# Attention and GELU MLP on one core: softmax denominators by way of a 96 x 16 reciprocal and DRAM, filler matmuls, and a reordered LayerNorm prologue

## The chip, the cores and the metric

The kernel runs on one core of one Trainium2 chip. The metric is device time in microseconds. A run more than 1.5% above the fastest of the same kernel is called slow. The rounds ran on chips 0, 3 and 8, so each ratio is to the kernel before in the same rounds, and medians of different rounds are compared only with care.

## The reference, cut to what matters

```python
x = A_x                                   # 1 x 2048 x 512
xn = _layernorm(x)
# attention: 32 heads of 16 for q, one shared k and v
p = softmax(einsum("bhqd,bkd->bhqk", q, k) * 16 ** -0.5)
o = einsum("bhqk,bkd->bhqd", p, v)
# MLP: 512 -> 1792 -> 512, gelu (tanh form), from the same xn
return x + merge_heads(o) @ wo + gelu(xn @ w1 + b1) @ w2 + b2
```

## The kernel before

Queries come in 4 blocks of 512, heads in 11 groups (ten of 3, one of 2), keys in 16 tiles of 128. That makes 4 x 11 x 16 = 704 steps. One step computes the scores of one key tile for the heads of a group, their exp, and the product with V:

```python
def scores(s):            # 17 active rows per head, heads side by side in row groups
    for j, h in enumerate(GROUPS[g]):
        mm(bank(3 * x + j), KT[q0:q0 + 17, ...], QT[q0:q0 + 17, ...], True, True, ..., tp=(q0, 0))
def exp(s):               # ACT, 128 x 1536
    act(lambda e: e.activation(E[:, s % NEB, 0:n * TBW], bank(3 * x, n), ACT.Exp, scale=0.25), ...)
def pv(s):                # 128 active rows, 32 columns per head, heads side by side in column groups
    for j, h in enumerate(GROUPS[g]):
        mm(pO[32 * j:32 * j + 32, :], V1[:, kt, :], E[:, s % NEB, ...], kt == 0, kt == NT - 1, ..., tp=(0, 32 * j))
```

V1 has a column of ones, so row 16 of each head's 32 rows of `pO` is its softmax denominator. After the 16th key tile the group is normalised. The first and the last instruction read `pO`, the reciprocal stands between them, and the next group's first product waits for all three:

```python
def o_evac(tb, g):
    n = 32 * len(GROUPS[g]); i = g % 2
    dve(lambda e: e.stream_shuffle(den[0:n, i, :], pO[0:n, :], [16] * 32), w=[B(6), ("den", i)])
    dve(lambda e: e.reciprocal(den[0:n, i, :], den[0:n, i, :]), r=[("den", i)], w=[("den", i)])
    dve(lambda e: e.tensor_tensor(oT[0:n, tb % 2, g, :], pO[0:n, :], den[0:n, i, :], ALU.mult),
        r=[("den", i)], w=[B(6), ("oT", tb % 2, g)])
```

The rest of the work (q of the next block, the MLP, the output projection) is a generator `misc()` of matmuls, of which the loop takes up to `PER_STEP = 2` per step. A block boundary yields "gap", and then the next step has none. I call a step with none of these matmuls an idle step.

```python
for s in range(NS):
    exp(s)
    if s + 2 < NS: scores(s + 2)
    pv(s)
    if kt == NT - 1: o_evac(tb, g); done[(tb, g)] = s
    # [cut: tanh of three MLP blocks on ACT when four are ready, gates two steps later]
    n = 0
    while mi_live and n < PER_STEP and s >= gap_until:
        k = next(mi)                      # [cut: end of the generator]
        if k == "gap": gap_until = s + 2
        else: n += 1
```

Of the kernel before, what the change touches and what calls it, by code (L numbers as in the profile page):

```python
# [7 lines left out]
ALU = mybir.AluOpType  # L8
AX = mybir.AxisListType

P = 128
# [101 lines left out]
def bass_parallel_sum__grouped_kv_mqa__dense_activation_gelu__prompt_kernel(  # L113
# [18 lines left out]
    H, Dh = 32, 16  # L132
    NT = S // P
    DT = D // P
    FT = F // P
    TBW = 512
    NTB = S // TBW
    GROUPS = [list(range(h, min(h + 3, H))) for h in range(0, H, 3)]
    NGR = len(GROUPS)
    NEB = 4  # L140
# [3 lines left out]
    with ExitStack() as es:  # L144
        def sb(shape, dtype, name):
            return es.enter_context(nc.sbuf_tensor(name, shape, dtype))
# [38 lines left out]
        sqq = sb([P, 2, TBW], bf, "sqq")  # L185
        mT = sb([32, 2, TBW], bf, "mT")
        E = sb([P, NEB, 3 * TBW], bf, "E")
        den = sb([96, 2, TBW], f32, "den")
        oT = sb([96, 2, NGR, TBW], bf, "oT")
        hb = sb([P, FT, TBW], bf, "hb")  # L190
        ub = sb([P, FT, TBW], bf, "ub")
# [5 lines left out]
        def bank(b, n=1):  # L197
            return pAll[:, b * 512:(b + n) * 512]
# [5 lines left out]
        def B(b):  # L204
            return ("bank", b)

        def dve(fn, r=(), w=()):
            return add("dve", fn, r, w)
# [4 lines left out]
        def pool(fn, r=(), w=()):  # L213
            return add("pool", fn, r, w)
# [14 lines left out]
        for i in range(8):  # L229
# [11 lines left out]
        pool(lambda e: e.affine_select(out=ident[:], in_=ident[:], compare_op=ALU.not_equal, fill=1.0, base=0,  # L241
                                       pattern=[[-1, P]], channel_multiplier=1), r=["ident"], w=["ident"])
        pool(lambda e: e.memset(wkp[:], 0.0), w=["wkp"])
        pool(lambda e: e.tensor_copy(wkp[:, :, :, 0:Dh], wk_s[:].unsqueeze(2).to_broadcast([P, DT, 4, Dh])),
             r=["wk_s", "wkp"], w=["wkp"])
        pool(lambda e: e.memset(mask4[:], 1.0), w=["mask4"])
        pool(lambda e: e.affine_select(out=mask4[:], in_=mask4[:], compare_op=ALU.is_ge, fill=0.0, base=0,
                                       pattern=[[-32, 4]], channel_multiplier=1), r=["mask4"], w=["mask4"])
# [2 lines left out]
        pool(lambda e: e.memset(ones[:], 1.0), w=["ones"])  # L251
        pool(lambda e: e.memset(sel8[:], 0.0), w=["sel8"])
        pool(lambda e: e.memset(selr[:], 0.0), w=["selr"])
        pool(lambda e: e.memset(V1[:], 0.0), w=["V1"])
        pool(lambda e: e.memset(V1[:, :, Dh:Dh + 1], 1.0), r=["V1"], w=["V1"])
        pool(lambda e: e.memset(wqp[:], 0.0), w=["wqp"])  # L256
        pool(lambda e: e.memset(wop[:], 0.0), w=["wop"])  # L257

        sel_diag = bass.AP(sel8[:].tensor, sel8[:].offset, [list(sel8[:].ap[0]), [33, 8], [8, 4]])

# [10 lines left out]
            dve(lambda e: e.tensor_copy(selr[:, :, 16:17], mask4[:].unsqueeze(2)), r=["mask4", "selr"], w=["selr"])  # L271


        def ln_batch(b):
            t0 = 4 * b
            for ti in range(t0, t0 + 4):
                dve(lambda e, ti=ti: e.bn_stats(stats[:, ti, :], x_sb[:, ti, :]), r=[("x", ti)], w=[("st", ti)])  # L277
            for ti in range(t0, t0 + 4):
                dve(lambda e, ti=ti: e.bn_aggr(mv[:, ti, :], stats[:, ti, :]), r=[("st", ti)], w=[("mv", b)])
            sl = slice(t0, t0 + 4)  # L280
            dve(lambda e: e.tensor_scalar(ve_b[:, sl], mv[:, sl, 1], 1e-5, None, ALU.add), r=[("mv", b)], w=[("ve", b)])
            act(lambda e: e.activation(std_b[:, sl], ve_b[:, sl], ACT.Sqrt), r=[("ve", b)], w=[("std", b)])
            dve(lambda e: e.tensor_copy(m_b[:, sl], mv[:, sl, 0]), r=[("mv", b)], w=[("mb", b)])
            dve(lambda e: e.reciprocal(rstd[:, sl], std_b[:, sl]), r=[("std", b)], w=[("rstd", b)])
            dve(lambda e: e.scalar_tensor_tensor(nmr[:, sl], m_b[:, sl], -1.0, rstd[:, sl], ALU.mult, ALU.mult),
                r=[("mb", b), ("rstd", b)], w=[("nmr", b)])
            for ti in range(t0, t0 + 4):
                if ti % 2 == 0:
                    act(lambda e, ti=ti: e.activation(xn[:, ti % 8, :], x_sb[:, ti, :], ACT.Identity,  # L289
                                                      bias=nmr[:, ti:ti + 1], scale=rstd[:, ti:ti + 1]),  # L290
                        r=[("x", ti), ("rstd", b), ("nmr", b)], w=[("xn", ti % 8)])
                else:
                    pool(lambda e, ti=ti: e.tensor_scalar(xn[:, ti % 8, :], x_sb[:, ti, :], rstd[:, ti:ti + 1],
                                                          nmr[:, ti:ti + 1], ALU.mult, ALU.add),
                         r=[("x", ti), ("rstd", b), ("nmr", b)], w=[("xn", ti % 8)])
                pT = bank(ti % 3)[:, 0:256].bitcast(bf)
                for d in range(DT):
                    add("pe", lambda e, ti=ti, d=d, pT=pT: e.transpose(  # L298
                        pT[:, d * P:(d + 1) * P], xn[:, ti % 8, d * P:(d + 1) * P], ident[:]),
                        r=[("xn", ti % 8), "ident"], w=[B(ti % 3)])  # L300
                act(lambda e, ti=ti, pT=pT: e.activation(  # L301
                    xnT[:, :, ti * P:(ti + 1) * P], pT.rearrange("p (k n) -> p k n", k=DT), ACT.Copy),
                    w=[B(ti % 3), ("xnT", b)])

        def k_block(b):
            bk = 3 + b % 2
            c = slice(b * TBW, (b + 1) * TBW)
            for d in range(DT):
                mm(bank(bk), wkp[:, d, :, :].rearrange("p a n -> p (a n)"), xnT[:, d, c], d == 0, d == DT - 1,
                   r=["wkp", ("xnT", b)], w=[B(bk)])  # L310
            act(lambda e: e.activation(KT[:, c], bank(bk), ACT.Identity, bias=krow[:, 0:1]),  # L311
                r=["krow"], w=[B(bk), ("KT", b)])
            dve(lambda e: e.tensor_tensor(sqk[:, b % 2, :], KT[0:Dh, c], KT[0:Dh, c], ALU.mult),
                r=[("KT", b)], w=[("sqk", b % 2)])
            mm(bank(5), ones[0:Dh, :], sqk[:, b % 2, :], True, True, r=["ones", ("sqk", b % 2)], w=[B(5)])
            dve(lambda e: e.tensor_reduce(kmax[:, b:b + 1], bank(5), AX.X, ALU.max), w=[B(5), "kmax"])
# [25 lines left out]
        def v_tiles(ts, first=False):  # L342
            for ti in ts:
                for d in range(DT):
                    mm(pO[:, ti * Dh:(ti + 1) * Dh], xnT[:, d, ti * P:(ti + 1) * P], wv_s[:, d, :], d == 0, d == DT - 1,
                       r=["wv_s", ("xnT", ti // 4)], w=[B(6)])

        ln_batch(0)
        consts_dve()
        ln_batch(1)  # L350
        k_block(0)
        dve(lambda e: e.tensor_copy(wqp[:, :, 0:8, 0:Dh], wq_s[:, :, 0:128].rearrange("p k (h n) -> p k h n", n=Dh)),
            r=["wq_s", "wqp"], w=["wqp"])
        ln_batch(2)
        k_block(1)
        ln_batch(3)
        q_first(0, 7)
        k_block(2)
        v_tiles(range(0, 12))
        k_block(3)  # L360
        dve(lambda e: e.tensor_reduce(R2[:], kmax[:], AX.X, ALU.max), r=["kmax"], w=["R2"])
        dve(lambda e: e.tensor_scalar(selrR[:], selr[:], R2[:, 0:1], 1.03, ALU.mult, ALU.mult),
            r=["selr", "R2"], w=["selrR"])
        q_first_m(0, 7)
        v_tiles(range(12, 16))
        q_first(1, 3)
        dve(lambda e: e.tensor_copy(V1[:, :, 0:Dh], pO[:, 0:NT * Dh].rearrange("p (t n) -> p t n", n=Dh)),
            r=["V1"], w=[B(6), "V1"])
# [21 lines left out]
        def pv(s):  # L390
            tb, g, kt = steps[s]
            for j, h in enumerate(GROUPS[g]):
                mm(pO[32 * j:32 * j + 32, :], V1[:, kt, :], E[:, s % NEB, j * TBW:(j + 1) * TBW],
                   kt == 0, kt == NT - 1, r=["V1", ("E", s % NEB)], w=[B(6)], tp=(0, 32 * j))

        def o_evac(tb, g):
            n = 32 * len(GROUPS[g])
            i = g % 2
            dve(lambda e: e.stream_shuffle(den[0:n, i, :], pO[0:n, :], [16] * 32), w=[B(6), ("den", i)])  # L399
            dve(lambda e: e.reciprocal(den[0:n, i, :], den[0:n, i, :]), r=[("den", i)], w=[("den", i)])  # L400
            dve(lambda e: e.tensor_tensor(oT[0:n, tb % 2, g, :], pO[0:n, :], den[0:n, i, :], ALU.mult),  # L401
                r=[("den", i)], w=[B(6), ("oT", tb % 2, g)])


        def q_batch(tb, hqs):
# [79 lines left out]
        def misc():  # L485
# [26 lines left out]
            for i in range(4):  # L512
                yield from part_tile(NTB - 1, i, range(LASTG))


        for j in range(3):
            n = len([g for g in GROUPS if len(g) > j])
# [7 lines left out]
        mi_live = True  # L525
        gap_until = 0
        gates = []

        scores(0)
        q_first_m(1, 3)  # L530
        scores(1)
        for s in range(NS):
            tb, g, kt = steps[s]
            exp(s)
            if s + 2 < NS:
                scores(s + 2)
            pv(s)
            if kt == NT - 1:
                o_evac(tb, g)
                done[(tb, g)] = s  # L540
            if tanh_ready and s >= gap_until and (len(tanh_ready) >= 4 or tanh_ready[-1] == FT - 1):
                fts = tanh_ready[:3] if tanh_ready[-1] != FT - 1 else tanh_ready[:3]
                del tanh_ready[:len(fts)]
                tanh(fts)
                gates.append((s + 2, fts))
            while gates and gates[0][0] <= s:
                gate(gates.pop(0)[1])
            n = 0
            while mi_live and n < PER_STEP and s >= gap_until:
                try:  # L550
                    k = next(mi)
                except StopIteration:
                    mi_live = False
                    break
                if k == "gap":
                    gap_until = s + 2
                else:
                    n += 1
        assert not gates and not tanh_ready
        for _ in mi:  # L560
            pass
# [39 lines left out]
```

## Time and profile before

| | before |
|---|---|
| median of 3 runs | 1356.33 us (1349.05 to 1361.22) |
| span of the profiled run | 1340.7 us |
| start to first exp / first to last exp / rest | 62.4 / 1259.4 / 18.9 us |
| mean granted TensorE clock | 0.578 of full |
| steps whose exp starts at half clock | 597 of 704 |

The page of the kernel before: span, busy time of the engines, the clock in 40 slices (tenths of full speed), and the chain of work that ended last, by engine and by line.

```profile
span 1340.7 us, 11668 instructions
PE 1061.3 (79%) x4964; PEld 208.6 (16%) x5029; DVE 447.0 (33%) x642; ACT 998.7 (74%) x758; POOL 17.4 (1%) x26
PEclk9655555555557865555556865555558655755557
PE 61%; ACT 19%; DVE 17%; issue 2%; POOL 1%; DMA 0%; DVEq 0%
```

No engine is full, and yet 97% of the chain lies on PE, ACT and DVE. The timeline of one group's end shows DVE's part. The columns are start in us, length in us, engine, line, operation and tiles; in brackets the idle time before and who ended it.

```profile
320.22 0.61 PE L222 MATMUL pAll<-E,V 128*32 128x512 bf16 x3
320.86 0.61 PE L222 MATMUL pAll<-QT,KT 17*128 17x512 bf16 x3
320.94 0.72 DVE L399 STREAM_SHUFFLE den<-pAll 96x512 f32<-96x512 f32 x1
321.70 3.35 DVE L400 RECIPROCAL den<-den 96x512 f32<-96x512 f32 x1
325.08 0.69 DVE L401 TENSOR_TENSOR oT<-pAll,den 96x512 bf16<-96x512 f32 x1
325.83 0.61 PE L222 MATMUL pAll<-E,V 128*32 128x512 bf16 x3 [4.36 <-DVE oT L401]
```

PE stands still for 4.36 us, because its next product needs the bank that DVE is still reading. The waits view has the total (us, times, longest):

```profile
ACT E L387 <- PE pAll L222: 277.1, 216, 4.6
PE pAll L222 <- DVE oT L401: 178.5, 43, 4.4
```

The second limit is the clock. This is a step with two other matmuls at half clock, PE alone:

```profile
395.71 0.61 PE L222 MATMUL pAll<-E,V 128*32 128x512 bf16 x3
396.26 1.03 PE L222 MATMUL pAll<-wop,oT 96*128 96x512 bf16 x2
397.23 0.61 PE L222 MATMUL pAll<-QT,KT 17*128 17x512 bf16 x3
397.77 0.61 PE L222 MATMUL pAll<-E,V 128*32 128x512 bf16 x3
```

From one product to the next it takes 397.77 - 395.71 = 2.06 us, and PE has no gap, while the exp of a step takes 1.45 us (median; it is 1.02 for the group of two heads). At full clock the same step is bound by ACT, at 1.33 us from exp to exp; here are five exps without a gap:

```profile
415.59 6.82 ACT L387 ACTIVATE E<-pAll 128x1536 bf16<-128x1536 f32 x5
```

ACT's own floor of the loop, worked out from exp spacings and tanh times of this trace, is 640 x 1.331 + 64 x 1.08 + 20 x 1.37 = 948 us; the loop takes 1259.

### The profile page before, as it was taken

The page shows a single profiled execution, that of the slowest core. Times are in us where ns is not written, and L with a number is a line of the kernel's source. Part 1 is how long each engine was busy: PE and PEld are TensorE (multiplying, and loading weights), DVE is VectorE, ACT ScalarE, POOL GpSimd, SP SyncE. Part 2 cuts the span into 40 slices and gives each one's busy share as a digit, 9 for nine tenths or more (in the row PEclk, how much of TensorE's full clock was granted, in tenths as well). Part 3 has the DMA queues.
Part 4 walks back from the last instruction along what each step waited for, and adds up shares of the span by engine and source line. Part 5 has one row for each costly group of instructions (what it writes and reads, how often), then busy time and mean ns, then how long its engine had stood idle before and what let it go on. Part 6 is the DMA issues. An engine that isn't in the chain of part 4 may idle for free.

```text
span 1340.7 us, 11668 instructions
## 1 busy us (share of the span) xinstructions
PE 1061.3 (79%) x4964; PEld 208.6 (16%) x5029; DVE 447.0 (33%) x642; ACT 998.7 (74%) x758; POOL 17.4 (1%) x26
## 2 busy tenths in 40 slices
PE   2588888788887888887888778888878888676788
PEld 1211111111111111111111111111111111111112
DVE  4323444432112135444311224443331113453112
ACT  3387778878867787787777867888878767877852
POOL 4000000000000000000000000000000000000000
PEclk9655555555557865555556865555558655755557
DMA  6000000000000000000000000000000000000000
GB/s 205 0 1 1 1 0 1 1 1 1 0 0 8 4 4 1 0 1 1 1 1 4 9 5 0 0 1 1 1 0 5 4 4 4 0 1 0 0 0 16
DMA packets 12882, 9.83 MB, mean 7 GB/s; under 512 B 5405, under 2 KB 12318, under 8 KB 12830
## 3 DMA queue, kind: packets, MB, share of 16 engines
q1 hardware_dynamic: 11774, 9.05, 2.2%
q8 instruction: 39, 0.64, 0.2%
q10 hardware_dynamic: 1056, 0.03, 0.0%
q14 instruction: 13, 0.11, 0.0%
HBM read 6.85 MB, written 2.10 MB: 7 GB/s over the span
## 4 chain that ended last, share of the span: by engine, by line
PE 61%; ACT 19%; DVE 17%; issue 2%; POOL 1%; DMA 0%; DVEq 0%
PE pAll L222 61%; ACT E L387 16%; DVE den L400 11%; DVE den L399 2%; DVE oT L401 2%; ACT ub L441 1%; PE pAll L298 0%; ACT xn L289 0%; ACT xnT L301 0%; POOL wop L257 0%; DVE stats L277 0%; DMA wk_s<-in_A_wk_dram 0%; POOL wqp L256 0%; ACT KT L311 0%; DVE outb L568 0%
## 5 line engine op out<-in xcount | busy, mean ns | idle before, releaser
L387 ACT ACTIVATE E<-pAll 128x1536 bf16<-128x1536 f32 (+1 forms) x704 | 953.8, 1425 | 285.9 <-PE pAll L222 277.1
L222 PE MATMUL pAll<-E,V 128*32 128x512 bf16 x2048 | 409.5, 575 | 178.5 <-DVE oT L401 178.5
L222 PE MATMUL pAll<-QT,KT 17*128 17x512 bf16 x2048 | 404.1, 567 | 39.3 <-ACT E L387 31.8
L400 DVE RECIPROCAL den<-den 96x512 f32<-96x512 f32 (+1 forms) x44 | 147.3, 3349 | 1.5
L222 PEld LDWEIGHTS pAll<-E,V 128*32 128x32 bf16 x2048 | 74.5, 100 | 466.0 <-issue 266.1
L222 PEld LDWEIGHTS pAll<-QT,KT 17*128 17x128 bf16 x2048 | 72.8, 97 | 464.4 <-ACT E L387 260.8
L222 PE MATMUL pAll<-xnT,w_sb 128*128 128x512 bf16 x196 | 102.3, 610 | 8.6 <-issue 8.6
L428 DVE TENSOR_SCALAR hb<-pAll,b1T 128x512 bf16<-128x512 f32 x56 | 42.0, 750 | 189.7 <-PE pAll L222 189.7
L222 PE MATMUL pAll<-w_sb,ub 128*128 128x512 bf16 x209 | 91.3, 534 | 5.4 <-issue 4.6
L399 DVE LOAD_MASK_SELECT den<-pAll x44 | 0.6, 14 | 240.3 <-PE pAll L222 240.3
L470 DVE TENSOR_TENSOR outb<-pAll,x_sb 128x512 bf16<-128x512 f32 x12 | 8.3, 692 | 178.4 <-PE pAll L222 178.4
L222 PE MATMUL pAll<-wop,oT 96*128 96x512 bf16 (+1 forms) x176 | 66.8, 468 | 0.0
L326 DVE CAST QT<-pAll 128x512 bf16<-128x512 f32 x32 | 22.1, 690 | 120.0 <-PE pAll L222 120.0
L222 PE MATMUL pAll<-xnT,wqp 128*128 128x512 bf16 x108 | 57.5, 621 | 3.7 <-issue 3.7
L413 DVE TENSOR_SCALAR mT<-pAll 32x512 int16<-32x512 int32 x30 | 20.4, 678 | 69.9 <-PE pAll L222 69.9
L446 DVE SCALAR_TENSOR_TENSOR ub<-ub,hb 128x512 bf16<-128x512 bf16 x56 | 35.4, 685 | 21.0 <-ACT ub L441 21.0
L298 PE MATMUL pAll<-ident,xn 128*128 128x128 bf16 x64 | 8.5, 310 | 33.2 <-ACT xn L289 29.8
L399 DVE STREAM_SHUFFLE den<-pAll 96x512 f32<-96x512 f32 (+1 forms) x44 | 31.7, 720 | 0.0
L401 DVE TENSOR_TENSOR oT<-pAll,den 96x512 bf16<-96x512 f32 (+1 forms) x44 | 30.2, 686 | 1.5
L441 ACT ACTIVATE ub<-ub 128x1536 bf16<-128x1536 bf16 (+1 forms) x20 | 27.9, 1393 | 0.1
L433 DVE TENSOR_TENSOR ub<-ub,hb 128x512 bf16<-128x512 bf16 x56 | 23.8, 426 | 1.9
L430 DVE TENSOR_TENSOR ub<-hb 128x512 bf16<-128x512 bf16 x56 | 23.8, 424 | 1.9
(69 smaller groups left out, 208.1 us busy)
## 6 DMA issues: line engine op xcount, KB each, us to landing
w_sb<-in_B_w_dram SPq DMA_DIRECT2D x2, 1792.0 KB, 12.5
x_sb<-in_A_x_dram SPq DMA_DIRECT2D x8, 256.0 KB, 4.5
out_dram<-outb SPq DMA_DIRECT2D x16, 128.0 KB, 1.7
QT<-mT SPq DMA_DIRECT2D x120, 1.0 KB, 1.6
wq_s<-in_A_wq_dram SPq DMA_DIRECT2D x1, 512.0 KB, 6.3
wop<-in_A_wo_dram SPq DMA_DIRECT2D x2, 176.0 KB, 5.5
wop<-in_A_wo_dram SPq DMA_DIRECT2D x1, 160.0 KB, 3.0
wk_s<-in_A_wk_dram ACTq DMA_DIRECT2D x1, 16.0 KB, 3.5
```

The costliest lines, as they stand in the source:

```text
L222: return add("pe", lambda e: e.matmul(o, l, rh, start=start, stop=stop, **kw), r, w)
L326: dve(lambda e: e.tensor_copy(QT[:, pq, hq, :], bank(bk)), w=[B(bk), ("QT", pq, hq)])
L387: act(lambda e: e.activation(E[:, s % NEB, 0:n * TBW], bank(3 * x, n), ACT.Exp, scale=0.25), w=[B(3 * x + i) for i in range(3)] + [("E", s ...
L399: dve(lambda e: e.stream_shuffle(den[0:n, i, :], pO[0:n, :], [16] * 32), w=[B(6), ("den", i)])
L400: dve(lambda e: e.reciprocal(den[0:n, i, :], den[0:n, i, :]), r=[("den", i)], w=[("den", i)])
L401: dve(lambda e: e.tensor_tensor(oT[0:n, tb % 2, g, :], pO[0:n, :], den[0:n, i, :], ALU.mult), r=[("den", i)], w=[B(6), ("oT", tb % 2, g)])
L413: dve(lambda e, hq=hq: e.tensor_scalar(mT[:, hq % 2, :].bitcast(i16), pM[0:32, :].bitcast(i32), 0.5 / 65536.0, float(0x1fc00000) / 65536.0 ...
L428: dve(lambda e: e.tensor_scalar(hb[:, ft, :], pM, b1T[:, ft:ft + 1], None, ALU.add), r=["b1T"], w=[B(7), ("h", ft)])
L430: dve(lambda e: e.tensor_tensor(ub[:, ft, :], hb[:, ft, :], hb[:, ft, :], ALU.mult), r=[("h", ft)], w=[("u", ft)])
L433: dve(lambda e: e.tensor_tensor(ub[:, ft, :], ub[:, ft, :], hb[:, ft, :], ALU.mult), r=[("u", ft), ("h", ft)], w=[("u", ft)])
L441: act(lambda e: e.activation(ub[:, f0:f0 + n, :], ub[:, f0:f0 + n, :], ACT.Tanh, scale=GELU_K), r=[("u", f) for f in fts], w=[("u", f) for ...
L446: dve(lambda e, ft=ft: e.scalar_tensor_tensor(ub[:, ft, :], ub[:, ft, :], 1.0, hb[:, ft, :], ALU.add, ALU.mult), r=[("u", ft), ("h", ft)], ...
```

## The change

The intent has three parts. Denominators: copy `pO` out in one instruction so that the bank is free, take the denominators of the group as 96 x 16 instead of 96 x 512 so that the reciprocal is short, and return them to all rows by DMA through DRAM. Fillers: bring each step to two matmuls so that PE stays busy and its clock up. Prologue: compute LayerNorm of the four batches without waiting for the key maximum, and keep long Pool memsets away from DVE copies (before, two copies took 3.89 and 3.37 us beside a memset of 4.82 us). It also has 12 matmuls that nobody reads (`warm`).

```diff
-def o_evac of before                    # [cut: shown above]
+def o_evac(tb, g):
+    dve(lambda e: e.tensor_copy(Of[0:32 * n, i, :], pO[0:32 * n, :]), w=[B(6), ("Of", i)])
+    row = Of[16:17, i, :]
+    dma("sp", den[0:32 * n, i, :], bass.AP(row.tensor, row.offset, [[32 * row.ap[0][0], n], [1, TBW]]), ...)
+def o_recip(tb, g):                     # 4 steps later
+    dve(lambda e: e.reciprocal(den[0:32 * n, i, :], den[0:32 * n, i, :]), ...)   # 96 x 16
+    dma("sp", rows, den[0:32 * n, i, :], f"d_rd{i}", ...)                        # to DRAM
+    for j in range(n):
+        dma("sp", rbc[32 * j:32 * j + 32, i, :], bass.AP(src.tensor, src.offset, [[0, 32], [1, TBW]]), ...)
+def o_norm(tb, g):                      # 10 steps later
+    dve(lambda e: e.tensor_tensor(oT[...], Of[...], rbc[...], ALU.mult), ...)
+def fill(s, n):
+    for _ in range(n):
+        mm(pO[96:128, :], V1[:, kt, :], E[:, s % NEB, 0:TBW], True, True, ..., tp=(0, 96))
 ...
             if kt == NT - 1:
                 o_evac(tb, g)
-                done[(tb, g)] = s
+                later.append((s + 4, ...o_recip...)); later.append((s + 10, ...o_norm, done...))
 ...
+            fill(s, PER_STEP - n)
 ...
-ln_batch(0); consts_dve(); ln_batch(1); k_block(0); <wqp copy>; ln_batch(2); k_block(1); ln_batch(3); ...
+ln_batch(0); x_T(0); ln_batch(1); x_T(1); consts_dve(); k_proj(0); ln_batch(2); x_T(2); k_proj(1); ln_batch(3); warm(8); x_T(3); warm(4); <wqp copy>; k_max(0); ...
```

The filler writes rows 96 to 127 of `pO`, which nobody reads.

More of the change, by code (lines that the diff above doesn't have):

```diff
@@ L187, in bass_parallel_sum__grouped_kv_mqa__dense_activation_gelu__prompt_kernel @@
         E = sb([P, NEB, 3 * TBW], bf, "E")
-        den = sb([96, 2, TBW], f32, "den")
+        Of = sb([96, 2, TBW], f32, "Of")
+        den = sb([96, 2, 16], f32, "den")
+        rbc = sb([96, 2, TBW], f32, "rbc")
+        rd_dram = nc.dram_tensor("rden_rows", [NTB * NGR, 3 * TBW], f32).ap()
         oT = sb([96, 2, NGR, TBW], bf, "oT")
@@ L243, in bass_parallel_sum__grouped_kv_mqa__dense_activation_gelu__prompt_kernel @@
         pool(lambda e: e.memset(wkp[:], 0.0), w=["wkp"])
-        pool(lambda e: e.tensor_copy(wkp[:, :, :, 0:Dh], wk_s[:].unsqueeze(2).to_broadcast([P, DT, 4, Dh])),
-             r=["wk_s", "wkp"], w=["wkp"])
         pool(lambda e: e.memset(mask4[:], 1.0), w=["mask4"])
@@ L253, in bass_parallel_sum__grouped_kv_mqa__dense_activation_gelu__prompt_kernel @@
         pool(lambda e: e.memset(selr[:], 0.0), w=["selr"])
-        pool(lambda e: e.memset(V1[:], 0.0), w=["V1"])
+        pool(lambda e: e.tensor_copy(wkp[:, :, :, 0:Dh], wk_s[:].unsqueeze(2).to_broadcast([P, DT, 4, Dh])),
+             r=["wk_s", "wkp"], w=["wkp"])
+        pool(lambda e: e.memset(V1[:, :, Dh:32], 0.0), w=["V1"])
         pool(lambda e: e.memset(V1[:, :, Dh:Dh + 1], 1.0), r=["V1"], w=["V1"])
-        pool(lambda e: e.memset(wqp[:], 0.0), w=["wqp"])
-        pool(lambda e: e.memset(wop[:], 0.0), w=["wop"])
+        dve(lambda e: e.memset(wqp[:, :, :, Dh:32], 0.0), w=["wqp"])
         sel_diag = bass.AP(sel8[:].tensor, sel8[:].offset, [list(sel8[:].ap[0]), [33, 8], [8, 4]])
@@ L271, in consts_dve, with ln_stats @@
             dve(lambda e: e.tensor_copy(selr[:, :, 16:17], mask4[:].unsqueeze(2)), r=["mask4", "selr"], w=["selr"])
+        def ln_stats(ti):
+            dve(lambda e: e.bn_stats(stats[:, ti, :], x_sb[:, ti, :]), r=[("x", ti)], w=[("st", ti)])
         def ln_batch(b):
             t0 = 4 * b
-            for ti in range(t0, t0 + 4):
-                dve(lambda e, ti=ti: e.bn_stats(stats[:, ti, :], x_sb[:, ti, :]), r=[("x", ti)], w=[("st", ti)])
+            for ti in range(t0 + (b > 0), t0 + 4):
+                ln_stats(ti)
             for ti in range(t0, t0 + 4):
@@ L283, in ln_batch @@
             dve(lambda e: e.tensor_copy(m_b[:, sl], mv[:, sl, 0]), r=[("mv", b)], w=[("mb", b)])
+            if b < 3:
+                ln_stats(t0 + 4)
             dve(lambda e: e.reciprocal(rstd[:, sl], std_b[:, sl]), r=[("std", b)], w=[("rstd", b)])
@@ L286, in ln_batch @@
                 r=[("mb", b), ("rstd", b)], w=[("nmr", b)])
+            on_act = [t0, t0 + 2] if b == 3 else [t0]
             for ti in range(t0, t0 + 4):
-                if ti % 2 == 0:
+                if ti in on_act:
                     act(lambda e, ti=ti: e.activation(xn[:, ti % 8, :], x_sb[:, ti, :], ACT.Identity,
@@ L295, in ln_batch, with warm, x_T @@
                          r=[("x", ti), ("rstd", b), ("nmr", b)], w=[("xn", ti % 8)])
-                pT = bank(ti % 3)[:, 0:256].bitcast(bf)
+        def warm(n):
+            for _ in range(n):
+                mm(bank(2), ident[:], xnT[:, 0, 0:TBW], True, True, r=["ident", ("xnT", 0)], w=[B(2)])
+        def x_T(b):
+            order = [4 * b, 4 * b + 1, 4 * b + 2, 4 * b + 3]
+            for ti in order:
+                bk = ti % 2
+                pT = bank(bk)[:, 0:256].bitcast(bf)
                 for d in range(DT):
@@ L299, in ln_batch, with k_proj @@
                         pT[:, d * P:(d + 1) * P], xn[:, ti % 8, d * P:(d + 1) * P], ident[:]),
-                        r=[("xn", ti % 8), "ident"], w=[B(ti % 3)])
+                        r=[("xn", ti % 8), "ident"], w=[B(bk)])
                 act(lambda e, ti=ti, pT=pT: e.activation(
                     xnT[:, :, ti * P:(ti + 1) * P], pT.rearrange("p (k n) -> p k n", k=DT), ACT.Copy),
-                    w=[B(ti % 3), ("xnT", b)])
-        def k_block(b):
+                    w=[B(bk), ("xnT", b)])
+        def k_proj(b):
             bk = 3 + b % 2
@@ L312, in k_block, with k_max @@
                 r=["krow"], w=[B(bk), ("KT", b)])
+        def k_max(b):
+            c = slice(b * TBW, (b + 1) * TBW)
             dve(lambda e: e.tensor_tensor(sqk[:, b % 2, :], KT[0:Dh, c], KT[0:Dh, c], ALU.mult),
@@ L348, in bass_parallel_sum__grouped_kv_mqa__dense_activation_gelu__prompt_kernel @@
         ln_batch(0)
+        x_T(0)
+        ln_batch(1)
+        x_T(1)
         consts_dve()
-        ln_batch(1)
-        k_block(0)
+        k_proj(0)
+        ln_batch(2)
+        x_T(2)
+        k_proj(1)
+        ln_batch(3)
+        warm(8)
+        x_T(3)
+        warm(4)
         dve(lambda e: e.tensor_copy(wqp[:, :, 0:8, 0:Dh], wq_s[:, :, 0:128].rearrange("p k (h n) -> p k h n", n=Dh)),
             r=["wq_s", "wqp"], w=["wqp"])
-        ln_batch(2)
-        k_block(1)
-        ln_batch(3)
+        k_max(0)
+        k_max(1)
+        k_proj(2)
+        k_proj(3)
         q_first(0, 7)
-        k_block(2)
-        v_tiles(range(0, 12))
-        k_block(3)
+        k_max(2)
+        k_max(3)
+        v_tiles(range(0, 16))
         dve(lambda e: e.tensor_reduce(R2[:], kmax[:], AX.X, ALU.max), r=["kmax"], w=["R2"])
@@ L364, in bass_parallel_sum__grouped_kv_mqa__dense_activation_gelu__prompt_kernel @@
         q_first_m(0, 7)
-        v_tiles(range(12, 16))
         q_first(1, 3)
@@ L396, in o_evac @@
         def o_evac(tb, g):
-            n = 32 * len(GROUPS[g])
-            i = g % 2
-            dve(lambda e: e.stream_shuffle(den[0:n, i, :], pO[0:n, :], [16] * 32), w=[B(6), ("den", i)])
-            dve(lambda e: e.reciprocal(den[0:n, i, :], den[0:n, i, :]), r=[("den", i)], w=[("den", i)])
-            dve(lambda e: e.tensor_tensor(oT[0:n, tb % 2, g, :], pO[0:n, :], den[0:n, i, :], ALU.mult),
-                r=[("den", i)], w=[B(6), ("oT", tb % 2, g)])
+            n = len(GROUPS[g])
+            i = (tb * NGR + g) % 2
+            dve(lambda e: e.tensor_copy(Of[0:32 * n, i, :], pO[0:32 * n, :]), w=[B(6), ("Of", i)])
+            row = Of[16:17, i, :]
+            dma("sp", den[0:32 * n, i, :], bass.AP(row.tensor, row.offset, [[32 * row.ap[0][0], n], [1, TBW]]),
+                f"d_den{i}", r=[("Of", i)], w=[("den", i)])
+        def o_recip(tb, g):
+            n = len(GROUPS[g])
+            i = (tb * NGR + g) % 2
+            rows = rd_dram[tb * NGR + g:tb * NGR + g + 1, 0:n * TBW]
+            dve(lambda e: e.reciprocal(den[0:32 * n, i, :], den[0:32 * n, i, :]), r=[("den", i)], w=[("den", i)])
+            dma("sp", rows, den[0:32 * n, i, :], f"d_rd{i}", r=[("den", i)], w=[("rd", i)])
+            for j in range(n):
+                src = rd_dram[tb * NGR + g:tb * NGR + g + 1, j * TBW:(j + 1) * TBW]
+                dma("sp", rbc[32 * j:32 * j + 32, i, :], bass.AP(src.tensor, src.offset, [[0, 32], [1, TBW]]),
+                    f"d_rb{i}{j}", r=[("rd", i)], w=[("rbc", i, j)])
+        def o_norm(tb, g):
+            n = len(GROUPS[g])
+            i = (tb * NGR + g) % 2
+            dve(lambda e: e.tensor_tensor(oT[0:32 * n, tb % 2, g, :], Of[0:32 * n, i, :], rbc[0:32 * n, i, :], ALU.mult),
+                r=[("Of", i)] + [("rbc", i, j) for j in range(n)], w=[("oT", tb % 2, g)])
+        def fill(s, n):
+            kt = steps[s][2]
+            for _ in range(n):
+                mm(pO[96:128, :], V1[:, kt, :], E[:, s % NEB, 0:TBW], True, True, r=["V1", ("E", s % NEB)], tp=(0, 96))
         def q_batch(tb, hqs):
@@ L513, in misc @@
                 yield from part_tile(NTB - 1, i, range(LASTG))
+        pool(lambda e: e.memset(wop[:], 0.0), w=["wop"])
         for j in range(3):
@@ L527, in bass_parallel_sum__grouped_kv_mqa__dense_activation_gelu__prompt_kernel @@
         gates = []
+        later = []
         scores(0)
@@ L537, in bass_parallel_sum__grouped_kv_mqa__dense_activation_gelu__prompt_kernel, with fin @@
             pv(s)
+            for d, fn in list(later):
+                if d <= s:
+                    fn()
+                    later.remove((d, fn))
             if kt == NT - 1:
                 o_evac(tb, g)
-                done[(tb, g)] = s
+                later.append((s + 4, lambda tb=tb, g=g: o_recip(tb, g)))
+                def fin(tb=tb, g=g, s=s):
+                    o_norm(tb, g)
+                    done[(tb, g)] = s
+                later.append((s + 10, fin))
             if tanh_ready and s >= gap_until and (len(tanh_ready) >= 4 or tanh_ready[-1] == FT - 1):
@@ L558, in bass_parallel_sum__grouped_kv_mqa__dense_activation_gelu__prompt_kernel @@
                     n += 1
+            fill(s, PER_STEP - n)
+        for d, fn in later:
+            fn()
         assert not gates and not tanh_ready
```

## The prediction

> **What bounds the kernel now.** The loop of 704 steps runs from 62.4 us (first exp, timeline) to 1321.8 of a 1340.7 us span. The chain of waits names PE 61%, ACT 19%, DVE 17%. Two things hold it above ACT's own rate.
> 1. At each of 43 group ends PE waits for the denominators: shuffle 0.72, reciprocal of 96x512 3.35, multiply 0.69 us. The waits view gives PE 178.5 us (43 times). The 43 gaps between exps take 232 us instead of 58: 174 us lost.
> 2. The granted clock averages 0.578. At half clock a step with two other matmuls takes 2.05 us and is PE-bound; 140 steps do. At full clock the same steps take 1.331 us, bound by ACT (timeline, 414-428 us). 140 x 0.72, and some at 1.55-1.8, are about 130 us.
> ACT's floor of the loop: 640 x 1.331 + 64 x 1.08 + 20 tanh x 1.37 = 948 us, against 1259 now.

> **What the change does.** Of 4.8 us at a group end one copy of 96x512 stays before PE may go on, about 0.72 us as the shuffle; the reciprocal shrinks to 96x16 (128x4 took 0.18); five small DMAs of about 2 us (1.0 KB landed in 1.6) have 4 and 6 steps (5.4 and 8 us) before anything needs them, so I expect them hidden. Gain: 4.1 x 43 = about 175 us where PE binds.
> Prologue: DVE copies that took 3.9 and 3.4 us beside the Pool memsets, and the wait of batches 2 and 3 behind the key maximum, go; first exp at about 40 us: -22. Tail: more output matmuls left: +4.

> **The clock decides the rest.** [...] only 0.5 and 1.0, changes at multiples of 3.41 us. [...] I expect falls in the h blocks and rises in stretches of two per step. Fillers cost PE at half clock: an idle step goes from 1.35 to about 1.5 us. All cold would be about 1365 us, all warm 1035. With a fifth to a third of the steps cold: loop about 1050.

> **Prediction:** 1110 us, range 1045 to 1215; faster by over 2%: 0.94, within 2%: 0.03, slower: 0.03. By step: stall -150 to -175, clock -60 to -110, prologue -15 to -25.

> **What would show it.** No PE wait over 1 us on DVE at group ends; reciprocal gone from the chain, exp (ACT) leading it with over half; mean clock 0.75 or more; exps 1.33 us apart; first exp near 40 us; DVE never waiting over 1 us for the broadcast DMAs.

> **What would make it wrong.** Clock staying near 0.58: fillers then lengthen steps and 100 us or less is gained. Fillers not streaming beside the value matmuls: cold steps cost 2.05 us[...]. The DMA chain taking over 8 us: DVE, in order, holds up evacuations that PE waits for. Fillers counting more than I think: nearly all warm, 1035-1050.

First exp near 40, loop about 1050, rest 18.9 + 4 come to about 1113, given as 1110. But that loop, and the -60 to -110 for the clock, stand as estimate; without the clock term the sum is 1163.

## The result

| | before | after |
|---|---|---|
| median of 4 runs | 1356.32 us (1349.05 to 1361.22) | 1158.38 us (1149.19 to 1195.35) |
| span of the profiled run | 1340.7 us | 1147.4 us |
| start to first exp / first to last exp / rest | 62.4 / 1259.4 / 18.9 us | 40.8 / 1079.3 / 27.2 us |
| mean granted clock, profiled run | 0.578 | 0.721 |
| steps whose exp starts at half clock | 597 of 704 | 378 of 704 |

The ratio is 0.8522 (95% interval 0.8437 to 0.8607). It is the mean time of one kernel's fast runs over that of the other's of the same rounds, so not quite the ratio of the medians. The run at 1195 us had clock 0.661.

The page of the changed kernel, the same lines:

```profile
span 1147.4 us, 13300 instructions
PE 1032.6 (90%) x5677; PEld 214.1 (19%) x5742; DVE 302.1 (26%) x599; ACT 998.1 (87%) x755; POOL 16.3 (1%) x28
PEclk9899676555559997665558998675556999675559
PE 57%; ACT 39%; DVE 1%; issue 1%; DMA 1%; POOL 0%; SPq 0%; DVEq 0%; ACTq 0%
```

DVE has left the chain. In exchange for 17% of 1341 us, ACT's share has doubled, but PE still leads. The clock has long stretches of 9 and long stretches of 5. A group's end (here that of the group of two heads), and the idle steps around it, at half clock:

```profile
583.31 1.04 PE L225 MATMUL pAll<-E,V 128*32 128x512 bf16 x4
583.99 0.68 DVE L428 COPY Of<-pAll 64x512 f32<-64x512 f32 x1 [3.46 <-PE pAll L225]
584.29 0.61 PE L225 MATMUL pAll<-QT,KT 17*128 17x512 bf16 x3
584.83 1.05 PE L225 MATMUL pAll<-E,V 128*32 128x512 bf16 x5
585.80 0.61 PE L225 MATMUL pAll<-QT,KT 17*128 17x512 bf16 x3
```

The copy fits beside the next scores, and PE waits for nothing visible. The five products of 584.83 are three heads and two fillers: 1.05 us where three alone took 0.61. From scores to scores it is 585.80 - 584.29 = 1.51 us. The waits view of the changed kernel, against that of before:

```profile
ACT E L416 <- PE pAll L225: 93.7, 147, 6.5
PEld pAll L225 <- DVE Of L428: 9.7, 30, 0.4
DVE oT L447 <- DMA rbc<-rden_rows: 59.7, 17, 4.6
```

The wait of PE's weight loads at group ends is at most 0.4 us. DVE was idle for up to 4.6 us before a multiply that the broadcast released.

In terms of the loop: the 43 gaps of over 3 us between exps, together 232 us before, are all gone. A gap held one step of 1.33 us anyway, so that is 232 - 43 x 1.33 = 175 us. The loop became 1259.4 - 1079.3 = 180 us shorter. **So by this count the stall accounts for 175, and everything else that happens in the loop, clock and fillers together, for only about 5.** e1 and e2 test it. The prologue gave 62.4 - 40.8 = 21.6 us and the tail took 8.3.

### Where the clock rises and falls

Of the falls in the changed kernel's loop I count the 16 after the first 45 us. Twelve have a tanh in the 6.83 us before them; here is one, at 729.6 us:

```profile
724.61 1.47 ACT L492 ACTIVATE ub<-ub 128x1536 bf16<-128x1536 bf16 x1
725.41 0.60 PE L225 MATMUL pAll<-xnT,w_sb 128*128 128x512 bf16 x2
727.47 0.39 PE L225 MATMUL pAll<-QT,KT 17*128 17x512 bf16 x3 [1.46 <-ACT E L416]
728.81 0.39 PE L225 MATMUL pAll<-QT,KT 17*128 17x512 bf16 x3
730.15 0.61 PE L225 MATMUL pAll<-QT,KT 17*128 17x512 bf16 x3 [0.40 <-ACT E L416]
```

ACT spends 1.47 us on the tanh, PE idles for 1.46 us, and three scores last 0.39 us before and 0.61 us after. The other four falls (87.9, 115.2, 688.7 and 958.3 us) come in runs of idle steps without a tanh; in the 3.41 us before that at 688.7 no gap of PE is over 0.41 us. After eight of the 12 falls at a tanh the clock is up again within 14 to 20 us, still in the MLP part. The other four come at the last two tanh of each block, 6.7 us apart, and there it stays down for 82 to 157 us, 471 us in all: of the 283 steps left 187 are idle. In the first three blocks it rises only when the output tiles have begun (second MLP products from 338.1, 607.0 and 876.7 us, rises at 340.5, 613.6 and 883.2), in the last one at 1118.7 us, at the end of the loop.

### The profile page after: what moved, and what is told of

Its sections match the earlier page's. It is cut to its first block, busy times and chain, and to the rows that moved or that the text cites. A ratio compares the mean times of both kernels' runs of the same rounds, so it can differ in the third digit from the quotient of the medians.

```text
span 1147.4 us, 13300 instructions
## 1 busy us (share of the span) xinstructions
PE 1032.6 (90%) x5677; PEld 214.1 (19%) x5742; DVE 302.1 (26%) x599; ACT 998.1 (87%) x755; POOL 16.3 (1%) x28
## 4 chain that ended last, share of the span: by engine, by line
PE 57%; ACT 39%; DVE 1%; issue 1%; DMA 1%; POOL 0%; SPq 0%; DVEq 0%; ACTq 0%
PE pAll L225 57%; ACT E L416 37%; ACT ub L492 2%; PE pAll L315 0%; ACT xnT L318 0%; DMA x_sb<-in_A_x_dram 0%; ACT xn L297 0%; DVE stats L277 0%; DVE outb L633 0%; DMA rbc<-rden_rows 0%; DMA den<-Of 0%; DMA rden_rows<-den 0%; DVE QT L346 0%; DVE kmax L336 0%; ACT KT L328 0%
## 5 line engine op out<-in xcount | busy, mean ns | idle before, releaser
L225 PE MATMUL pAll<-E,V 128*32 128x512 bf16 x2749 | 486.0, 513 | 0.0
L225 PE MATMUL pAll<-QT,KT 17*128 17x512 bf16 x2048 | 354.7, 495 | 69.8 <-ACT E L416 52.2
L225 PEld LDWEIGHTS pAll<-E,V 128*32 128x32 bf16 x2749 | 83.6, 99 | 240.0 <-issue 229.3
L428 DVE COPY Of<-pAll 96x512 f32<-96x512 f32 (+1 forms) x44 | 30.2, 686 | 255.8 <-PE pAll L225 255.8
L225 PE MATMUL pAll<-xnT,w_sb 128*128 128x512 bf16 x196 | 79.7, 485 | 6.4 <-issue 6.2
L225 PE MATMUL pAll<-w_sb,ub 128*128 128x512 bf16 x209 | 70.5, 428 | 9.1 <-DVE xpy L530 6.0
L225 PE MATMUL pAll<-wop,oT 96*128 96x512 bf16 (+1 forms) x176 | 54.5, 396 | 0.0
L447 DVE TENSOR_TENSOR oT<-Of,rbc 96x512 bf16<-96x512 f32 (+1 forms) x44 | 30.1, 683 | 59.7 <-DMA rbc<-rden_rows 59.7
L437 DVE RECIPROCAL den<-den 96x16 f32<-96x16 f32 (+1 forms) x44 | 10.8, 245 | 55.3 <-DMA den<-Of 54.9
L225 PEld LDWEIGHTS pAll<-w_sb,ub 128*128 128x128 bf16 x224 | 14.5, 101 | 37.0 <-issue 27.7
```

The source lines that it names most:

```text
L225: return add("pe", lambda e: e.matmul(o, l, rh, start=start, stop=stop, **kw), r, w)
L428: dve(lambda e: e.tensor_copy(Of[0:32 * n, i, :], pO[0:32 * n, :]), w=[B(6), ("Of", i)])
L437: dve(lambda e: e.reciprocal(den[0:32 * n, i, :], den[0:32 * n, i, :]), r=[("den", i)], w=[("den", i)])
L447: dve(lambda e: e.tensor_tensor(oT[0:32 * n, tb % 2, g, :], Of[0:32 * n, i, :], rbc[0:32 * n, i, :], ALU.mult), r=[("Of", i)] + [("rbc", i ...
```

## The experiments

Theory A: the stall at the group ends is the main gain; the fillers, as they are, gain at full clock about what they cost at half. Rival B: the fillers carry much of the gain through the clock. Rival C: it is the short reciprocal that counts. Then, for the clock: the rows that stream decide (row theory, a guess), against "PE busy decides" (E) and "tanh and stalls decide, not idle steps" (D). All twelve runs gave a correct result.

### e1: denominators alone

```diff
 kernel before
-o_evac with shuffle, reciprocal 96x512, multiply
+o_evac / o_recip / o_norm of the change; no fillers, prologue of before
```

> The kernel before with the denominator path of the change alone (copy out, 96x16 reciprocal, return by DMA; no fillers, prologue as before). Theory A (the group-end stall is the main gain; the clock and fillers decide the rest): no PE wait over 1 us at group ends, 43 x 4.1 = 175 us gone, so about 1180 us (1150 to 1200), granted clock between 0.55 and 0.7, first exp near 62 us. Rival B (the gain needs the fillers; without them the clock stays at 0.58 and PE-bound steps use up much of what the stall gave): 1230 us or more.

Measured: 1171.66 us (1171.50, 1171.59, 1201.23, 1171.74), ratio 0.8645; clock 0.602; first exp at 62.2 us; no gap over 3 us between exps. As theory A said. Of the 198 us between the medians of before and after, this part alone gives 186.

### e2: the changed kernel without fillers

```diff
 kernel after
-            fill(s, PER_STEP - n)
```

> The changed kernel without the fillers of the loop (prologue and denominators as changed). Theory A: 1145 us (1120 to 1175), that is e1 minus 22 us; clock below 0.721 of the changed kernel but idle steps at 1.35 us instead of 1.52 at half clock, so within 3% of the changed kernel: the fillers gain in one place about what they cost in another. Rival B (fillers carry a large part of the gain through the clock): 1200 us or more.

Measured: 1160.83 us (1148.34, 1152.68, 1168.98, 1174.37), ratio 0.8489; clock 0.608. The changed kernel had 0.8522, and 0.8756 when run again (e12). **About 700 fillers raised the clock from 0.61 to 0.72 and bought nothing** (by e12 they may have cost a little). The loop from first to last exp says the same: 1077.5 us in e1, 1075.2 here, 1079.3 with the fillers. In the traces: without fillers 120 steps take the 2.05 us of a step with two at half clock, with them 84; but 227 steps take about 1.51 us, against 32 without. Rival B falls.

### e3: fillers alone

```diff
 kernel before
+            fill(s, PER_STEP - n)
```

> The kernel before with the fillers alone (denominators and prologue as before). Theory A: the 4.4 us stalls stay and drop the clock each time; idle steps at half clock cost 0.17 us more, some 300 of them: 1340 to 1400 us, no faster than before. Rival B (fillers lift the clock by themselves): 1300 us or less, clock 0.65 or more.

Measured: 1405.80 us (1398.65 to 1407.56), ratio 1.0355: slower. The upper edge of the range was slightly passed. The clock did rise, to 0.621. A higher mean clock is not a gain in itself.

### e4: prologue of before

```diff
 kernel after
-reordered prologue
+prologue of before
```

> Denominators and fillers as changed, prologue as before. The prologue is an additive 22 us (first exp 62.4 against 40.8 us): 1180 us, first exp at 62 us. If the prologue mattered through the clock of the loop, the difference would be well off 22 us, beyond the scatter of some 20 us that the changed kernel shows.

Measured: 1209.34 us median (1207.42, 1211.26, 1176.12, 1213.17); first exp at 62.3 us. Against the two sets of the changed kernel, 1158.38 and 1194.56, the difference is 15 to 51 us, and the scatter of either is some 30 us. The start to the first exp, 62.3 against 40.8 to 42.1 us, shows the 20 to 22 us; whether the loop's clock also changes is not settled by these runs. At the same mean clock, 0.716, e4 took 1176.12 us and the changed kernel 1152.83, so 23 us. e1 and e2, which differ only in the prologue, say 0.8645 against 0.8489, that is 0.0156 x 1357 = 21 us.

### e5: denominators kept on the chip

```diff
 kernel after
-DMA of the rows to 96x16; reciprocal 96x16; DMA to DRAM; broadcast DMA
+dve: stream_shuffle(rbc, Of, [16]*32); reciprocal(rbc, rbc)      # 96x512, 4 steps later
```

> The changed kernel, but the denominators stay on the chip: the copy out of the bank is kept, then DVE itself spreads (0.72 us) and takes the reciprocal of 96x512 (3.35 us) from the copy, 4 steps later, and multiplies 10 steps later; no DMA. Theory A (what counted was to free the bank early; the reciprocal's size and the DMA route matter little): within 2% of the changed kernel, 1140 to 1185 us; PE's wait at group ends stays under 1 us; DVE about 4 us per group busier. Rival C (the small reciprocal is what counts; a 4 us DVE block in order holds up the evacuations): 1200 us or more, long waits of PE for the bank of the other matmuls.

Measured: 1154.90, 1183.22, 1184.22, 1187.56 us; clock 0.688 in the first. Within the span of the changed kernel's runs, so theory A is not contradicted; but the scatter of the clock hides differences under 3%. e10 repeats this with the clock held.

### e6: a third filler in idle steps

The guess: the first filler of an idle step streams in the free columns beside the three products and does nothing for the clock. Its time fits that in e9, with 0.62 us for four products against 0.61 for three.

```diff
 kernel after
-            fill(s, PER_STEP - n)
+            fill(s, PER_STEP - n + (n == 0))
```

> The changed kernel with a third filler in every step that has no other matmul. Row theory (first filler streams beside the value matmuls and counts nothing[...]): an idle step [...] at half clock behaves as one with two others (2.05 us[...]), so clock 0.85 or more and 1085 us (1060 to 1130). Rival D (the low clock is set by tanh and stalls, not by idle steps): the third filler only lengthens cold steps: 1180 us or more, clock unchanged near 0.70.

Measured: 1042.38 us (1041.02 to 1044.12), ratio 0.7738. The time came out 18 us below the lower edge of the range of theory, because the clock, 0.965, did better than "0.85 or more":

```profile
PE 900.7 (87%) x6071; PEld 237.8 (23%) x6071; DVE 301.3 (29%) x599; ACT 970.5 (93%) x755; POOL 16.2 (2%) x28
PEclk9799989999999999899999999899999999989998
ACT 81%; PE 13%; DMA 3%; DVE 2%; issue 0%; SPq 0%; POOL 0%; DVEq 0%; ACTq 0%
```

There are 329 more matmuls than in the changed kernel, one for each idle step (6071 against 5742 by the weight loads; the trace of the changed kernel lacks 65 matmul records), and yet 132 us less busy PE (1032.6 - 900.7): at full clock each takes less time (three scores 0.39 us instead of 0.61). ACT leads the chain. Rival D falls: a filler more in the idle steps alone raised the clock from 0.721 to 0.965. And the scatter is gone (3 us).

### e7: the same fillers with 32 active rows

```diff
 e6
-mm(pO[96:128, :], V1[:, kt, :],    E[:, s % NEB, 0:TBW],    True, True, ..., tp=(0, 96))
+mm(pO[96:128, :], V1[0:32, kt, :], E[0:32, s % NEB, 0:TBW], True, True, ..., tp=(0, 96))
```

> As the third-filler kernel, with the same filler matmuls of the same 512 columns but only 32 active rows. Row theory: [...] the clock is no better than without fillers in idle steps while they cost the same PE time: clock 0.62 or less, 1190 us or more. Rival E (what counts is PE being busy, whatever the rows): clock and time as the third-filler kernel, within 2%.

Measured: 1549.02 us (1546.36 to 1552.64), ratio 1.1494, worse than any other.

```profile
PE 1515.8 (98%) x6071; PEld 298.9 (19%) x6071; DVE 300.9 (19%) x599; ACT 1023.2 (66%) x755; POOL 16.2 (1%) x28
PEclk9555555555555895555555695555555559555557
```

PE is busy for 98% of the span and the clock is 0.571; in e6 it was busy for 87% at 0.965. So the busy share of the profile does not tell the clock, and rival E falls. One part of my expectation was wrong: "the same PE time". Two idle steps of e7:

```profile
605.09 2.00 PE L225 MATMUL pAll<-E,V 128*32 128x512 bf16 x6
607.02 0.61 PE L225 MATMUL pAll<-QT,KT 17*128 17x512 bf16 x3
607.56 2.00 PE L225 MATMUL pAll<-E,V 128*32 128x512 bf16 x6
609.49 0.61 PE L225 MATMUL pAll<-QT,KT 17*128 17x512 bf16 x3
```

609.49 - 607.02 = 2.47 us: by the time that they take, all three fillers stream after the products, none beside them; no run shows why. So e7 also pays more PE time per idle step than e6 would at half clock, and part of its 1549 us is that. The clock is told apart all the same: 0.570 to 0.576 in the four runs with 32-row fillers, 0.954 to 0.965 with 128-row ones. That rows weigh in proportion, and against which level, is not shown.

### e8: more fillers where a tanh is issued

```diff
 e6
-            fill(s, PER_STEP - n + (n == 0))
+            fill(s, PER_STEP - n + (n == 0) + 4 * tanhed)     # tanhed: this step issued a tanh
```

> The third-filler kernel with four more fillers in each of the 20 steps that issue a tanh. Row theory: [...] falls at tanh go: clock 0.92 or more, 1065 us (1045 to 1095), and about 20 us better than the third-filler kernel. Rival: if falls have another cause, no gain over it.

Measured: 1031.10 us (1026.41 to 1032.56), ratio 0.7644; clock 0.986, and 8 of 704 steps at half clock. The gain over e6 is 11 us, not 20: e6 already fell less often than I assumed, with 33 steps at half clock. The loop is now 960 us, against the floor of 948.

```profile
PEclk9789999999999999999999999999999999999998
ACT 86%; PE 9%; DVE 2%; DMA 2%; SPq 0%; issue 0%; POOL 0%; DVEq 0%; ACTq 0%
```

### e9: one filler, in idle steps alone

```diff
 kernel after
-            fill(s, PER_STEP - n)
+            fill(s, 1 if n == 0 else 0)
```

> The changed kernel with one filler, and only in steps that have no other matmul. If the first filler streams beside the value matmuls and neither costs PE time nor counts for the clock: same as the kernel without fillers (e2: 1161 us, clock 0.61, idle step at half clock 1.35 us), 1140 to 1180 us, clock 0.58 to 0.64. Rival: it counts as any filler does: clock 0.68 or more, or idle steps of 1.5 us at half clock.

Measured: 1172.76, 1159.68, 1109.15, 1153.44 us; clocks 0.578, 0.602, 0.645, 0.598. Median 1156.56, as without fillers; one run at 1109 us lies outside the range that I gave, with the highest clock. An idle step at half clock, from the run of 1172.76:

```profile
592.55 0.61 PE L225 MATMUL pAll<-QT,KT 17*128 17x512 bf16 x3 [0.18 <-ACT E L416]
593.09 0.62 PE L225 MATMUL pAll<-E,V 128*32 128x512 bf16 x4
593.89 0.61 PE L225 MATMUL pAll<-QT,KT 17*128 17x512 bf16 x3 [0.18 <-ACT E L416]
```

Three products and a filler take 0.62 us, as three take 0.61, and the step is 1.34 us. The first filler costs no time, and in three of four runs this kernel cannot be told from the one without any in clock and time.

### e10: e8 with the denominators kept on the chip

```diff
 e8
-DMA route, reciprocal 96x16
+shuffle and reciprocal 96x512 on DVE from the copy, as in e5
```

> The kernel of e8 (third filler, more at tanh) with the denominators of e5 (copied out, then 96x512 reciprocal on DVE, no DMA). With the clock steady the route itself shows. Theory A (freeing the bank early is what counts): within 2% of e8's 1031 us, 1025 to 1050 us. Rival C (the 3.35 us block on DVE delays evacuations that PE waits for): 1065 us or more.

Measured: 1024.55 us (1023.11 to 1026.23), ratio 0.7599 (0.7577 to 0.7621), clock 0.988. It is the fastest of all and beats both kernels. Its interval touches that of e8 (0.7620 to 0.7668), so "no slower" is shown, and that it is faster by the 6.6 us between the medians is not.

```profile
L432 DVE RECIPROCAL rbc<-rbc 96x512 f32<-96x512 f32 (+1 forms) x44 | 147.3, 3349 | 1.5
```

The reciprocal still takes 3.35 us 44 times, 147 us of DVE, and costs nothing: rival C falls, and the round trip through DRAM was not needed.

### e11: e8 with the denominators of before

```diff
 e8
-o_evac / o_recip / o_norm of the change
+o_evac of before
```

> The kernel of e8 with the denominators of before (4.8 us on the critical path at each group end). Additive in time: 43 x about 3.8 = 165 us, 1195 us, clock 0.9 or more. If the stall also drops the clock each time [...]: some 5 to 8 us of half clock after each, so 1230 to 1330 us and clock 0.6 to 0.8.

Measured: 1323.67 us (1321.54 to 1324.57), ratio 0.9815, clock 0.79. That is the second branch of what I wrote: not 165 us but 293 more than e8. 44 gaps of over 3 us take 245 us, 186 more than steps would; and 200 steps are at half clock. Only the stall of PE, about 4 us at each of 43 group ends, is different from e8, and the clock is 0.794 against 0.986 there.

```profile
ACT E L413 <- PE pAll L222: 293.6, 228, 6.8
PEld pAll L222 <- DVE oT L427: 184.0, 43, 4.5
```

### e12: the changed kernel again

> The changed kernel again, beside these: 1150 to 1195 us, clock 0.66 to 0.73, scattered as before [...].

Measured: 1172.34, 1200.13, 1188.99, 1200.44 us, clocks 0.687, 0.651, 0.672, 0.651; ratio 0.8756 (0.8677 to 0.8836). The runs at lower clocks took longer.

## Why the prediction was right

The predicted range, 1045 to 1215 us around 1110, holds the measured 1158, and the direction was right. Part of this is luck. The range is 170 us wide, and without any gain by the clock the other terms give 1356 - 175 - 22 + 4 = 1163, which it holds as well. By step:

- **Stall, predicted -150 to -175: right.** 175 us in the loop; -186 us for that part alone (e1).
- **Prologue, predicted -15 to -25, first exp near 40 us: right.** 40.8 us; 21.6 us.
- **Tail, predicted +4:** 8.3 us. A small miss.
- **Clock, predicted -60 to -110: wrong in size.** It gave about 5. The step that failed is "With a fifth to a third of the steps cold": 378 of 704, 54%, were. The parts were as predicted: 12 of the 16 falls come at a tanh, an idle step at half clock went from 1.35 to 1.51 us (predicted about 1.5), the first filler of an idle step costs no time (0.62 us for four products, 0.61 for three, e9). But I counted on rises "in stretches of two per step". They came within 20 us after eight of the 12 falls at a tanh, but not after the last two tanh of a block: there mostly idle steps remain (187 of 283), the clock stays at 0.5 for 82 to 157 us, and the fillers only lengthen the steps. These four stretches hold 283 of the 378 cold steps. A second miss took back part of the first: on my line from 1035 us (all warm) to 1365 (all cold) a cold step costs 330 / 704 = 0.47 us, and with 54% of the steps cold it gives 1212, where the profiled run took 1149: in its trace exps are 1.66 us apart at half clock and 1.39 at full, a difference of 0.27. This term of the sum was off by some 55 us or more, against a miss of 48 us in the total.
- **Signs:** no PE wait over 1 us at group ends, right (0.4). Reciprocal gone from the chain, right. Exp leading the chain with over half, wrong (ACT 39%, PE 57%). Clock of 0.75 or more, wrong (0.721, and 0.651 to 0.716 in other runs). Exps 1.33 us apart, for 309 of 703. DVE never waiting over 1 us for the broadcast DMAs, wrong: it waited 17 times, 16 of them over 1 us, up to 4.6. I had counted steps between the issue and the need as time, and DVE does not wait for steps: where nothing else stands between the reciprocal and the multiply in its order, it goes on to the multiply at once and waits for the write to DRAM and the broadcast. So it is in the 12 waits of over 4 us; here is one.

```profile
290.93 0.69 DVE L428 COPY Of<-pAll 96x512 f32<-96x512 f32 x1 [11.55 <-PE pAll L225]
293.70 0.25 DVE L437 RECIPROCAL den<-den 96x16 f32<-96x16 f32 x1 [2.08 <-DMA den<-Of]
298.28 0.69 DVE L447 TENSOR_TENSOR oT<-Of,rbc 96x512 bf16<-96x512 f32 x1 [4.33 <-DMA rbc<-rden_rows]
```

  The five shorter waits (0.56 to 2.85 us) have small query-row DMAs ahead of the broadcast in the SP queue. All of it costs little: replacing the whole route changed the median by 6.6 us (e10 against e8).
- Of the alternatives that I listed as "would make it wrong", one was itself wrong: with the clock staying near 0.6, e1 and e2 still gained 186 and 197 us, not 100 or less. "All warm 1035" is what e6 and e8 came near, by a third filler and not because fillers count more.

The parts do not add. Removing the stall is worth 186 us with the clock of before, and 293 us with enough fillers. The fillers of e8 are worth 1161 - 1031 = 130 us without the stall, and with it almost nothing: e11 is at 0.9815, where before minus a prologue of 21 us would be at 0.984. Removing the stall pays by itself; the fillers need the stall removed, and the change has one too few of them per idle step to get that.

I leave open why the clock in one run of e9 stayed up longer than in the others, and whether the prologue acts on the loop's clock (e4).

## What to carry to other kernels

When a wait ends at a buffer, free the buffer first and do the slow arithmetic later on the copy; making the arithmetic fast was not needed here. Fillers must be judged by the clock that they hold and by the steps that they lengthen, both measured. Here one filler per idle step took no time and left the clock at 0.578 to 0.645 (e9; 0.580 to 0.608 without fillers, e2), and 32-row fillers left it at 0.571 where 128-row ones gave 0.965 (e7, e6). A half-measure can cost about what it gains; here one more filler per idle step turned about 0 us into 116 (medians of e6 and of the first four runs of the changed kernel).
